# An adaLN block in split fp32: weight work of one pair of f tiles and a row scaling at later points, sums and splits interleaved, and another order of the last token tiles

## The chip, the cores and the metric

The kernel runs on one core of one Trainium2 chip. Its time is the device time of one execution, in microseconds (us). Five engines matter here: TensorE (PE, the matmuls; PEld is its weight loading), VectorE (DVE), ScalarE (ACT), GpSimd (POOL) and SyncE (SP), whose queue issues every DMA of this kernel. Each engine takes its instructions in the order in which they were written and waits, on semaphores, for what an instruction needs; whatever stands behind a waiting instruction on its engine waits too.

## The reference, cut to what matters

A token block of 2048 rows by 512 columns goes through a conditioned layer norm, linear attention, a second layer norm and a bilinear feed-forward network. The change touches the network's last part only:

```python
g = jnp.einsum("bsd,df->bsf", x, w_gate)      # 512 -> 1376
u = jnp.einsum("bsd,df->bsf", x, w_up)
h = g * u
return jnp.einsum("bsf,fd->bsd", h, w_down)   # 1376 -> 512
...
x = x + gb * _B_ref(h, B_w_gate, B_w_up, B_w_down)
```

Here `gb` is a row of 512 numbers. The kernel scales the rows of `w_down` by it once, so that the product needs only to be added to `x`.

## The kernel before, in words

**Tiling.** The 2048 tokens are four chunks of four token tiles (128 rows each); the 1376 columns f are ten tiles of 128 and one of 96, tile 10, which the code calls odd. Everything is fp32, and a matmul takes fp32r operands: each operand is split into a rounded part, written by ACT (`AF.Copy`), and the remainder, a subtraction on DVE or POOL. A product of two split operands is three matmuls. A split is thus ACT first, then DVE or POOL, and both parts go to PE.

**The network** handles two chunks at a time with a seven-product scheme for 2x2 blocks (Strassen-Winograd), so that blocks are summed and subtracted before they are split. `block` (L1174) makes one f tile of h for two chunks in seven products over four PSUM banks a, b, c, d, with 42 matmuls of 512 columns. Between products it calls what is planned for the points p1, p5, p6, p2, p7, p3, p4, in that order in time. The sum at L1218 (`p5 = c + p5`) reads bank c after the fifth product, and the seventh product writes c again, so PE has the length of the sixth product for it.

**The last eleven steps** (numbers 8 to 18 of the network; called step 0 to step 10 here) make h for chunks 2 and 3, in the order f = 10, 8, 9, 0 to 7. Step 0 is the odd tile; steps 1 and 2 are the first pair of f tiles, steps 3 and 4 the second, and so on, five pairs. In the first steps the leftover down products of earlier groups run too, with their sums into x (L943) and stores.

**Weight work.** During these steps `Down.planned` (L1450) prepares `w_down`: for each pair the two raw tiles are loaded (`w_load`), scaled by `gb` (`w_scale`, L1366, DVE), combined into t1 to t4 (`w_sum`, L1380, four subtractions of 256 columns on DVE), split (`w_parts`, L1357 on ACT and L1358 on POOL) and stored to DRAM (`w_park`, SP), since SBUF has no room for all; `w_fetch` brings them back. The line `put(b, point, ...)` names step and point. The odd tile's rows are scaled at L1455 on DVE.

**The last stage**, `Down.run` (L1477), makes the seven products of the second matmul for both chunks. PE works in products of two token tiles (`lo`, `hi`); each token tile takes five pairs times three matmuls of 256 columns, and three more where the odd tile belongs to the product. Two token tiles share one PSUM bank. `add` (L1485, DVE) adds a finished tile to x, and stores follow. The sums of h (`h_sum`, L1413, DVE) and their splits (L196 ACT, L197 DVE) are written between the products; `h_next` does sum and split pair by pair for s2 and s4, where s4 needs s2.

**Buffers.** All tiles in SBUF come from one pool of 94 buffers (`tiles`, L64), given out in the order of the program; a buffer's new user waits for the last readers and writers of the old one. The order is written out by hand: no scheduler moves an instruction.

## Time and profile before

| | |
|---|---|
| median of 3 runs | 543.92 us (543.61 to 544.06) |
| the profiled execution | 543.86 us |
| its span, first to last instruction | 542.2 us |
| PE busy | 535.5 us, 99% of the span |
| DVE, ACT, POOL busy | 407.4, 295.9, 160.7 us |
| DMA | 109.21 MB, mean 201 GB/s |

The span starts 0 at the first instruction; a row of the timeline gives start, length, engine, source line, operation and tiles. A row for several matmuls (x16) starts with the first. A matmul's length in such rows includes its way through the array, during which the next one has already started; so the distance between starts tells what a matmul costs, and that is 0.12 us for one of 256 columns and 0.227 us for one of 512 (17 starts from 388.01 to 391.86).

### The profile page before, as it was taken

To read this page: it belongs to the slowest core of one execution; us is meant where nothing else is said; L and a number is where in the kernel's file an instruction comes from. 1 tells how busy PE (TensorE), PEld (TensorE's weight loads), DVE (VectorE), ACT (ScalarE), POOL (GpSimd) and SP (SyncE) were. 2 spreads that over 40 slices of the span, in tenths; PEclk is the share of its full clock that TensorE was granted. 3 is DMA by queue.
4 is the path that set the end of the run, shared out by engine and by line. 5 is a ranking of instruction groups with operands and counts; after the bars stand their busy time and mean duration, and the time that the engine had idled before them with its cause. 6 is when DMAs were issued, how large, how long until landed. Compare 5 with 4: busy or idle time off the path is not lost. (4 is left out here: it accounts for less than half of the span.)

```text
span 542.2 us, 8140 instructions
## 1 busy us (share of the span) xinstructions
PE 535.5 (99%) x2617; PEld 448.3 (83%) x2617; DVE 407.4 (75%) x688; ACT 295.9 (55%) x557; POOL 160.7 (30%) x169
## 2 busy tenths in 40 slices
PE   8999999999999999999999999999999999999997
PEld 7888787888888878878888888887788888899996
DVE  7897779999989888779765677997745554666762
ACT  3696777648587765577674545444524234353320
POOL 2001010010021220085796566749622313210000
PEclk9999999999999999999999999999999999999999
DMA  8902427220165165947879496893189999689122
GB/s 280 383 35 98 136 93 218 89 68 2 44 195 196 37 213 154 294 142 237 285 215 314 186 318 207 254 371 95 43 299 375 380 382 325 224 296 365 52 79 78
DMA packets 86395, 109.21 MB, mean 201 GB/s; under 512 B 10896, under 2 KB 41616, under 8 KB 86352
## 3 DMA queue, kind: packets, MB, share of 16 engines
q1 hardware_dynamic: 86352, 108.70, 59.8%
q8 instruction: 20, 0.33, 0.2%
q14 instruction: 23, 0.19, 0.1%
HBM read 65.93 MB, written 42.73 MB: 200 GB/s over the span
## 5 line engine op out<-in xcount | busy, mean ns | idle before, releaser
L1156 PE MATMUL bank<-h,w 128*128 128x512 f32 (+1 forms) x630 | 145.7, 390 | 0.4 <-DVE u L1218 0.3
L1156 PEld LDWEIGHTS bank<-h,w 128*128 128x128 f32 (+1 forms) x630 | 116.9, 186 | 27.1 <-DVE u L1218 0.7
L1161 ACT ACTIVATE bank<-bank 128x512 f32<-128x512 f32 (+1 forms) x30 | 17.5, 583 | 73.8 <-PE bank L1156 73.6
L197 DVE TENSOR_TENSOR kl<-u,kh 128x512 fp32r<-128x512 f32 (+1 forms) x43 | 30.6, 743 | 27.8 <-ACT kh L196 23.7
L265 POOL TENSOR_TENSOR rstd<-ve,half 128x2 f32<-128x2 f32 (+3 forms) x13 | 11.8, 910 | 109.0 <-DVE ve L264 45.0
L211 PE MATMUL bank<-w,h 128*128 128x512 f32 x104 | 40.9, 393 | 0.1
L209 PE MATMUL bank<-w,h 128*128 128x512 f32 x104 | 40.9, 393 | 0.0
L210 PE MATMUL bank<-w,h 128*128 128x512 f32 x104 | 40.6, 390 | 0.0
L1156 PE MATMUL acc<-h,w 128*128 128x512 f32 x168 | 38.7, 389 | 0.0
L197 POOL TENSOR_TENSOR w<-raw,w 128x512 fp32r<-128x512 f32 (+1 forms) x15 | 21.6, 1446 | 53.4 <-ACT w L196 47.7
L873 PE MATMUL acc<-w,xh 128*128 128x512 f32 x120 | 37.1, 390 | 0.0
L1156 PEld LDWEIGHTS acc<-h,w 128*128 128x128 f32 x168 | 31.5, 188 | 6.5
L1118 POOL TENSOR_TENSOR w<-raw,w 128x256 fp32r<-128x256 f32 (+3 forms) x22 | 24.8, 1127 | 38.3 <-ACT w L1111 34.1
L943 DVE TENSOR_TENSOR x<-acc,x 128x512 f32<-128x512 f32 x40 | 26.1, 685 | 9.9 <-PE acc L1241 8.2
L1436 PE MATMUL acc<-w,kh 128*128 128x256 f32 (+1 forms) x176 | 31.9, 284 | 0.1
L1118 POOL TENSOR_TENSOR w<-t,w 128x512 fp32r<-128x512 f32 (+1 forms) x22 | 29.9, 1357 | 0.0
L196 ACT ACTIVATE kh<-u 128x512 fp32r<-128x512 f32 (+1 forms) x43 | 24.6, 622 | 8.3 <-DVE u L1413 8.3
L1436 PEld LDWEIGHTS acc<-w,kh 128*128 128x128 f32 (+1 forms) x176 | 27.5, 192 | 0.4 <-ACT kh L196 0.3
L873 PEld LDWEIGHTS acc<-w,xh 128*128 128x128 f32 x120 | 22.5, 188 | 4.6
L416 PE MATMUL acc<-kh,xh 128*128 128x512 f32 x64 | 25.3, 395 | 0.0
L1436 PE MATMUL acc<-w,kl 128*128 128x256 f32 x88 | 25.0, 284 | 0.2 <-DVE kl L197 0.2
L1436 PE MATMUL bank<-w,kh 128*128 128x256 f32 (+1 forms) x136 | 24.7, 284 | 0.5 <-DVE x L1485 0.5
(257 smaller groups left out, 1330.0 us busy)
## 6 DMA issues: line engine op xcount, KB each, us to landing
right<-w SPq DMA_DIRECT2D x56, 256.0 KB, 3.4
w<-right SPq DMA_DIRECT2D x56, 256.0 KB, 5.1
raw<-in_w_mod_dram SPq DMA_DIRECT2D x24, 256.0 KB, 3.7
raw<-in_B_w_down_dram SPq DMA_DIRECT2D x20, 256.0 KB, 4.4
down_t<-w SPq DMA_DIRECT2D x20, 256.0 KB, 5.1
w<-down_t SPq DMA_DIRECT2D x20, 256.0 KB, 4.2
x<-in_A_x_dram SPq DMA_DIRECT2D x16, 256.0 KB, 5.4
down_b<-w SPq DMA_DIRECT2D x15, 256.0 KB, 5.2
```

The costliest lines, as they stand in the source:

```text
L196: nc.scalar.activation(h, src, AF.Copy)
L197: (low or nc.vector).tensor_tensor(l, src, f32(h), op=ALU.subtract)
L209: nc.tensor.matmul(ps, ah, bh, start=i == 0, stop=False)
L210: nc.tensor.matmul(ps, ah, bl, start=False, stop=False)
L211: nc.tensor.matmul(ps, al, bh, start=False, stop=i == n - 1)
L416: nc.tensor.matmul(tacc[k], xh[:, a:b], kh, start=first, stop=False)
L873: nc.tensor.matmul(yps[i], x, y, start=False, stop=k == KD - 1 and x is al, skip_group_check=True)
L943: nc.vector.tensor_tensor(xt[:, a:b], dn[j][:, a:b], xt[:, a:b], op=ALU.add)
L1118: sub = lambda out, x, y: (on or nc.gpsimd).tensor_tensor(out, x, f32(y), op=ALU.subtract)
L1156: mm = lambda x, y, **kw: nc.tensor.matmul(ps, x[:, k], y, skip_group_check=True, **kw)
L1161: nc.scalar.activation(out, x, AF.Copy)
L1436: nc.tensor.matmul(ps, x[:, a:b], y, start=start, stop=False, skip_group_check=True)
```

## The change

Four things are written differently; what is computed is the same, and so is the number of instructions on every engine.

1. The odd tile's scaling (L1455) goes from point p6 of step 0 to point p6 of step 1.
2. For the first pair only (`i == 0`), the weight work stands later. The sums go from p7 of step 1 to p6 of step 2; the split of b11 and b21 from p3 of step 1 to p1 of step 2; that of b22 and t1 from p4 of step 1 to p7 of step 2; that of t2, t3, t4 from p6 and p7 to p4 of step 2. The four stores of b11, b21, b22 and t1 go from p1 and p2 of step 2 to its p4. On SP's queue they keep their place: behind the seven loads of the network's weights for step 3, ahead of the two raw tiles of the second pair.
3. `h_next` writes the next pair's sum ahead of the current pair's remainder on DVE, and from s2's last pair goes over to the first sum of s4.
4. The last product takes token tiles 0, 2, 1, 3 instead of 0, 1, 2, 3, and a tile's sum into x is written behind the next tile's product.

```diff
--- before.py
+++ after.py
@@ -1341,6 +1341,8 @@
 
     HALF = D // 2
 
+    FOLLOWS = {"s2": "s4"}
+
     class Down:
 
         def __init__(self, cs, m, odd):
@@ -1419,9 +1421,19 @@
                 self.parts.setdefault(i, {})[name, "split"] = h, l
 
         def h_next(self, name, *pairs):
+
+            self.ahead(name, pairs[0])
             for i in pairs:
+                h, l = B("kh", dt=F32R), B("kl", dt=F32R)
+                x = self.a(i, name)
+                nc.scalar.activation(h, x, AF.Copy)
+                self.ahead(*((name, i + 1) if i + 1 < self.NI else (FOLLOWS.get(name), 0)))
+                nc.vector.tensor_tensor(l, x, f32(h), op=ALU.subtract)
+                self.parts[i][name, "split"] = h, l
+
+        def ahead(self, name, i):
+            if name and name not in self.parts[i]:
                 self.h_sum(name, i)
-                self.h_split(name, i)
 
         def part(self, bs, j):
             return bs[j // 2][:, j % 2 * HALF:(j % 2 + 1) * HALF]
@@ -1452,20 +1464,26 @@
             def put(b, point, *does):
                 plan.setdefault((self.m + b, point), []).extend(does)
 
-            put(0, "p6", lambda: nc.vector.tensor_tensor(self.odd, self.odd, gb[:self.odd.shape[0]], op=ALU.mult))
+            put(1, "p6", lambda: nc.vector.tensor_tensor(self.odd, self.odd, gb[:self.odd.shape[0]], op=ALU.mult))
             put(1, "p4", *(lambda n=n: self.w_split(("odd", n), self.odd[:, n * HALF:(n + 1) * HALF], nc.gpsimd) for n in range(2)))
             for i in range(self.NI):
                 a, b = 1 + 2 * i, 2 + 2 * i
                 put(a - 1, "p4", lambda i=i: self.w_load(i))
                 put(a, "p1", lambda i=i: self.w_scale(i))
-                put(a, "p7", lambda i=i: self.w_sum(i, "t1", "t3", "t2", "t4"))
-                put(a, "p3", lambda i=i: self.w_parts(i, "b11", "b21"))
-                put(a, "p4", lambda i=i: self.w_parts(i, "b22", "t1"))
-                put(b, "p1", lambda i=i: self.w_park(i, "b11", "b21"))
                 put(b, "p5", lambda i=i: self.h_split("a11", i))
-                put(b, "p6", lambda i=i: self.w_parts(i, "t2", "t3"))
-                put(b, "p2", lambda i=i: self.w_park(i, "b22", "t1"))
-                put(b, "p7", lambda i=i: self.w_parts(i, "t4"))
+                if i:
+                    put(a, "p7", lambda i=i: self.w_sum(i, "t1", "t3", "t2", "t4"))
+                    put(a, "p3", lambda i=i: self.w_parts(i, "b11", "b21"))
+                    put(a, "p4", lambda i=i: self.w_parts(i, "b22", "t1"))
+                    put(b, "p1", lambda i=i: self.w_park(i, "b11", "b21"))
+                    put(b, "p6", lambda i=i: self.w_parts(i, "t2", "t3"))
+                    put(b, "p2", lambda i=i: self.w_park(i, "b22", "t1"))
+                    put(b, "p7", lambda i=i: self.w_parts(i, "t4"))
+                else:
+                    put(b, "p1", lambda i=i: self.w_parts(i, "b11", "b21"))
+                    put(b, "p6", lambda i=i: self.w_sum(i, "t1", "t3", "t2", "t4"))
+                    put(b, "p7", lambda i=i: self.w_parts(i, "b22", "t1"))
+                    put(b, "p4", lambda i=i: self.w_parts(i, "t2", "t3", "t4"), lambda i=i: self.w_park(i, "b11", "b21", "b22", "t1"))
                 if i + 1 < self.NI:
                     put(b + 1, "p1", lambda i=i: self.w_park(i, "t2", "t3", "t4"))
                     put(b + 1, "p5", lambda i=i: self.h_sum("s1", i))
@@ -1545,9 +1563,12 @@
             for j in range(NJ):
                 self.mm(O, j, odd, j % 2 == 0)
             add(c1, 1, O, range(NJ), (HALF, D))
-            for js in (lo, (2,), (3,)):
-                self.product(Y, js, "a22", "t4", False, (1, 0))
-                add(c1, 0, Y, js, (0, HALF))
+            before = []
+            for j in (0, 2, 1, 3):
+                self.product(Y, (j,), "a22", "t4", False, (1, 0))
+                add(c1, 0, Y, before, (0, HALF))
+                before = (j,)
+            add(c1, 0, Y, before, (0, HALF))
 
     def fill(n):
         for _ in range(n):
```

Engine order, first place: DVE in steps 0 and 1. In the kernel before, the odd tile's scaling (L1455, tile raw with row) stands behind the last remainder (h) written ahead of it and in front of the sum L1218 of step 0:

```order
L197 TENSOR_TENSOR h_4187<-f_3822,h_4186 128x512
L1455 TENSOR_TENSOR raw_4067<-raw_4067,row_1562 96x512
L1218 TENSOR_TENSOR u_4184<-bank_2867,u_4184 96x512
L1222 TENSOR_TENSOR u_4197<-bank_2868,u_4197 96x512
L1184 TENSOR_TENSOR u_4197<-bank_2865,u_4197 96x512
L1184 TENSOR_TENSOR u_4184<-bank_2867,u_4184 96x512
```

and the first pair's sums (L1380, tiles t) stand in step 1, behind L1218 and ahead of L1222:

```order
L1218 TENSOR_TENSOR u_4309<-bank_2867,u_4309 128x512
L1380 TENSOR_TENSOR t_4348<-raw_4255 128x256
L1380 TENSOR_TENSOR t_4349<-raw_4257,raw_4255 128x256
L1380 TENSOR_TENSOR t_4348<-raw_4257,t_4348 128x256
L1380 TENSOR_TENSOR t_4349<-raw_4257,t_4348 128x256
L1222 TENSOR_TENSOR u_4318<-bank_2868,u_4318 128x512
L1184 TENSOR_TENSOR u_4318<-bank_2865,u_4318 128x512
L1184 TENSOR_TENSOR u_4309<-bank_2867,u_4309 128x512
```

Now step 1 has the odd scaling (L1467) behind the pair's two scalings, and no sums:

```order
L1368 TENSOR_TENSOR raw_4254<-raw_4254,row_1562 128x512
L1368 TENSOR_TENSOR raw_4256<-raw_4256,row_1562 128x512
L1467 TENSOR_TENSOR raw_4067<-raw_4067,row_1562 96x512
L1218 TENSOR_TENSOR u_4308<-bank_2867,u_4308 128x512
L1222 TENSOR_TENSOR u_4317<-bank_2868,u_4317 128x512
L1184 TENSOR_TENSOR u_4317<-bank_2865,u_4317 128x512
L1184 TENSOR_TENSOR u_4308<-bank_2867,u_4308 128x512
```

and the sums (L1382) stand in step 2, behind the remainder of the split of a11 (kl) and ahead of that step's L1218:

```order
L197 TENSOR_TENSOR kl_4432<-u_4317,kh_4431 128x512
L1382 TENSOR_TENSOR t_4444<-raw_4254 128x256
L1382 TENSOR_TENSOR t_4445<-raw_4256,raw_4254 128x256
L1382 TENSOR_TENSOR t_4444<-raw_4256,t_4444 128x256
L1382 TENSOR_TENSOR t_4445<-raw_4256,t_4444 128x256
L1218 TENSOR_TENSOR u_4429<-bank_2867,u_4429 128x512
L1222 TENSOR_TENSOR u_4442<-bank_2868,u_4442 128x512
L1184 TENSOR_TENSOR u_4442<-bank_2865,u_4442 128x512
L1184 TENSOR_TENSOR u_4429<-bank_2867,u_4429 128x512
```

One row moved by a step, and four rows moved by a step and from behind L1218 to ahead of it.

Second place: DVE in the last stage, at the start of `h_next` for s2 (tiles s are the sums, kl the remainders, x rows the adds). Before, sum and remainder of a pair follow each other:

```order
L1413 TENSOR_TENSOR s_4564<-s_4564,u_4318 128x512
L197 TENSOR_TENSOR kl_5436<-s_4564,kh_5435 128x512
L1413 TENSOR_TENSOR s_4750<-s_4750,u_4573 128x512
L197 TENSOR_TENSOR kl_5441<-s_4750,kh_5440 128x512
L1485 TENSOR_TENSOR x_156<-x_156,acc_4525 128x256
L1485 TENSOR_TENSOR x_158<-x_158,acc_4525 128x256
L1413 TENSOR_TENSOR s_4936<-s_4936,u_4759 128x512
L197 TENSOR_TENSOR kl_5478<-s_4936,kh_5477 128x512
L1413 TENSOR_TENSOR s_5122<-s_5122,u_4945 128x512
L197 TENSOR_TENSOR kl_5483<-s_5122,kh_5482 128x512
L1485 TENSOR_TENSOR x_160<-x_160,acc_4526 128x256
L1485 TENSOR_TENSOR x_162<-x_162,acc_4526 128x256
```

Now the sum of the next pair stands ahead of the remainder of the current one:

```order
L1415 TENSOR_TENSOR s_4564<-s_4564,u_4317 128x512
L1415 TENSOR_TENSOR s_4750<-s_4750,u_4573 128x512
L1431 TENSOR_TENSOR kl_5436<-s_4564,kh_5435 128x512
L1415 TENSOR_TENSOR s_4936<-s_4936,u_4759 128x512
L1431 TENSOR_TENSOR kl_5441<-s_4750,kh_5440 128x512
L1503 TENSOR_TENSOR x_156<-x_156,acc_4525 128x256
L1503 TENSOR_TENSOR x_158<-x_158,acc_4525 128x256
L1415 TENSOR_TENSOR s_5122<-s_5122,u_4945 128x512
L1431 TENSOR_TENSOR kl_5478<-s_4936,kh_5477 128x512
L1415 TENSOR_TENSOR s_5279<-s_5279,u_5131 128x512
L1431 TENSOR_TENSOR kl_5483<-s_5122,kh_5482 128x512
L1503 TENSOR_TENSOR x_160<-x_160,acc_4526 128x256
```

Every remainder has moved down by one sum; the adds keep their places among the remainders.

Third place: DVE at the end (x_156, x_158, x_160 and x_162 are token tiles 0 to 3 of chunk 3; bank_2865 holds tiles 0 and 1, bank_2866 tiles 2 and 3). Before:

```order
L1485 TENSOR_TENSOR x_162<-x_162,bank_2868 128x256
L1485 TENSOR_TENSOR x_156<-x_156,bank_2865 128x256
L1485 TENSOR_TENSOR x_158<-x_158,bank_2865 128x256
L1485 TENSOR_TENSOR x_160<-x_160,bank_2866 128x256
L1485 TENSOR_TENSOR x_162<-x_162,bank_2866 128x256
```

Now:

```order
L1503 TENSOR_TENSOR x_162<-x_162,bank_2868 128x256
L1503 TENSOR_TENSOR x_156<-x_156,bank_2865 128x256
L1503 TENSOR_TENSOR x_160<-x_160,bank_2866 128x256
L1503 TENSOR_TENSOR x_158<-x_158,bank_2865 128x256
L1503 TENSOR_TENSOR x_162<-x_162,bank_2866 128x256
```

The middle two adds have changed places, as the products on PE have; each add now stands behind the product of the following tile in the program.

## The prediction

> **What bounds the kernel now.** I read the head of the page first, then who waits for whom on PE, then PE's timeline where it waits.
>
> ```profile
> PE 535.5 (99%) x2617; PEld 448.3 (83%) x2617; DVE 407.4 (75%) x688; ACT 295.9 (55%) x557; POOL 160.7 (30%) x169
> ```
>
> PE is busy for 99% of the span, so nothing but PE's own waits can be won by a new order. The view of waits, cut to PE, names all of them:
>
> ```profile
> PE acc L146 <- DVE w L141: 2.0, 1, 2.0
> PE bank L1436 <- DVE x L1485: 0.5, 1, 0.5
> PE bank L1156 <- DVE u L1218: 0.3, 1, 0.3
> PE acc L1436 <- DVE kl L197: 0.2, 1, 0.2
> PE bank L1156 <- DVE u L1184: 0.2, 1, 0.2
> ```
>
> The first is the start of the program, which the change doesn't touch. The other four each happen once, all for DVE, and add up to 1.2 us of idle PE. That counts only time in which no matmul is in the array; what PE loses in starts is more. In its timeline the four stand here:
>
> ```profile
> 368.79 3.85 PE L1156 MATMUL bank<-h,w 128*96 128x512 f32 x16
> 372.90 1.63 PE L1156 MATMUL bank<-h,w 128*96 128x512 f32 x6 [0.26 <-DVE u L1218]
> 374.36 0.40 PE L1239 MATMUL acc<-w,kh 128*128 128x512 f32 x1
> ...
> 391.86 0.39 PE L1241 MATMUL acc<-w,kl 128*128 128x512 f32 x1
> 392.43 3.91 PE L1156 MATMUL bank<-h,w 128*128 128x512 f32 x16 [0.18 <-DVE u L1184]
> ...
> 512.50 0.28 PE L1436 MATMUL acc<-w,kl 128*128 128x256 f32 x1
> 512.87 0.50 PE L1436 MATMUL acc<-w,kh 128*128 128x256 f32 x2
> 513.60 0.39 PE L1436 MATMUL acc<-w,kl 128*128 128x256 f32 x1 [0.23 <-DVE kl L197]
> 513.82 0.40 PE L1436 MATMUL acc<-w,kh 96*128 96x256 f32 x2
> ...
> 535.66 0.28 PE L1436 MATMUL bank<-w,kl 96*128 96x256 f32 x1
> 536.45 0.50 PE L1436 MATMUL bank<-w,kh 128*128 128x256 f32 x2 [0.51 <-DVE x L1485]
> 536.79 0.28 PE L1436 MATMUL bank<-w,kl 128*128 128x256 f32 x1
> ```
>
> Sixteen matmuls of 512 columns take 3.85 us with the last one's 0.40, so a start comes every 3.45 / 15 = 0.23 us; of 256 columns every 0.40 - 0.28 = 0.12 us. By these:
>
> - Gap 1, step 0: 372.90 - 368.79 - 16 x 0.23 = 0.43, and the six behind it take 1.46 in place of 1.38: 0.08. Together 0.51 us.
> - Gap 2, end of step 1: 392.43 - 391.86 - 0.23 = 0.34 us.
> - Gap 3, product s4: four starts from 512.50 to 513.82 take 1.32 in place of 0.48: 0.84 us.
> - Gap 4, last token tile: three starts from 535.66 to 536.79 take 1.13 in place of 0.36: 0.77 us.
>
> The sum is 2.46 us. It is what the change can win at most, and each of its four parts stands at one gap.
>
> **The change part by part.** DVE's rows in steps 0 to 3:
>
> ```profile
> 371.02 1.22 DVE L1455 TENSOR_TENSOR raw<-raw,row 96x512 f32<-96x512 f32 x1
> 372.17 0.68 DVE L1218 TENSOR_TENSOR u<-bank,u 96x512 f32<-96x512 f32 x1
> ...
> 382.51 1.28 DVE L1366 TENSOR_TENSOR raw<-raw,row 128x512 f32<-128x512 f32 x2
> 385.59 0.69 DVE L1218 TENSOR_TENSOR u<-bank,u 128x512 f32<-128x512 f32 x1 [1.79 <-PE bank L1156]
> 386.20 1.56 DVE L1380 TENSOR_TENSOR t<-raw 128x256 f32<-128x256 f32 x1
> ...
> 389.12 1.84 DVE L1380 TENSOR_TENSOR t<-raw,t 128x256 f32<-128x256 f32 x2
> ...
> 396.68 0.69 DVE L197 TENSOR_TENSOR kl<-u,kh 128x512 fp32r<-128x512 f32 x1 [2.00 <-issue]
> 399.55 0.69 DVE L1218 TENSOR_TENSOR u<-bank,u 128x512 f32<-128x512 f32 x1 [2.18 <-PE bank L1156]
> ...
> 407.19 1.40 DVE L1366 TENSOR_TENSOR raw<-raw,row 128x512 f32<-128x512 f32 x2 [1.51 <-DMA raw<-in_B_w_down_dram]
> ...
> 411.86 0.69 DVE L1218 TENSOR_TENSOR u<-acc,u 128x512 f32<-128x512 f32 x1 [1.94 <-PE acc L1156]
> 412.47 0.48 DVE L1380 TENSOR_TENSOR t<-raw 128x256 f32<-128x256 f32 x1
> ...
> 413.20 1.34 DVE L1380 TENSOR_TENSOR t<-raw,t 128x256 f32<-128x256 f32 x2
> ```
>
> *The odd scaling.* It ran 1.22 us right ahead of the L1218 that PE waited for; without it L1218 can start up to 1.15 us earlier, at 371.0, ends near 371.8, and PE wants it at 372.90 - 0.43 = 372.47. Gap 1 goes: -0.51 us. At its new place DVE is idle for 1.79 us ahead of L1218; the scaling costs 0.64 there (half of 1.28), at most the 1.22 of its old row. Covered: 0. Without that cover it would cost its length less 1.79, so nothing either way.
>
> *The first pair's sums.* They ran from 386.20 to 389.12 + 1.84 = 390.96, 4.76 us, ahead of L1222 and the two L1184, for which PE waited at 392.43. Without them L1222 and L1184 run when PE releases them. Gap 2 goes: -0.34 us. In step 2 the sums now stand between the remainder that ends at 396.68 + 0.69 = 397.37 and L1218, in a hole of 2.18 us. Their price there isn't in the trace; the nearest rows are those of the second pair, which ran from 412.47 to 413.20 + 1.34 = 414.54: 2.07 us. The other end is the first pair's own 4.76. Behind them wait L1218 and, through it, PE's seventh product. L1218 starts when the fifth product has left the array; the sixth takes 6 x 0.23 = 1.38, L1218 itself 0.69, and the last matmul of the fifth stays about 0.40 - 0.23 = 0.17 in the array beyond its share, so L1218 may be 0.5 us late before PE notices (an estimate from these rows). Sums of up to 2.18 + 0.5 = 2.7 us are thus free. Which end applies is told by POOL and ACT:
>
> ```profile
> 387.44 1.47 POOL L1118 TENSOR_TENSOR w<-t,w 128x512 fp32r<-128x512 f32 x1
> ...
> 398.30 2.14 POOL L1358 TENSOR_TENSOR w<-t,w 128x256 fp32r<-128x256 f32 x3 [4.65 <-ACT w L1357]
> ```
>
> ```profile
> 395.47 0.60 ACT L1161 ACTIVATE u<-bank 128x512 f32<-128x512 f32 x1 [0.74 <-PE bank L1156]
> ...
> 397.80 1.03 ACT L1357 ACTIVATE w<-t 128x256 fp32r<-128x256 f32 x3
> ```
>
> Where the sums were slow, POOL worked on remainders of 512 columns. Where they go, POOL was idle for 4.65 us up to 398.30, since ACT has no rounded part for it before 397.80, and now this is the time of b22 and t1 (p7). Two of POOL's remainders, b11 and b21, are new ahead of it: they follow ACT's two new splits at p1, which fill ACT's idle 0.74 ahead of 395.47 (three splits take 1.03, two about 0.7), so POOL ends them near 397. The sums meet POOL only from 398.30 on, as the second pair's do; I take 2.07, and the cost is 0. The trace thus has 1.56 beside POOL's 1.47, and 0.48 for the same operation apart from it. The Trainium skill, "SBUF — State Buffer", section "Who interferes with whom", says why: a VectorE instruction with two SBUF inputs and a GpSimd instruction that reads SBUF use one port, and whichever starts second is blocked until the other has finished. By my row the cost here is 0; by the strict form of that rule it is the 0.6 us of the second rival below.
>
> *Splits and stores.* ACT has b22, t1, t2, t3, t4 (five, 0.31 apart) from 397.80 on, in place of three: 0.7 us more, with no PE work of ACT's behind it in that step. POOL ends five remainders of 2.14 / 3 = 0.71 near 398.3 + 3.6 = 401.9. SP's queue:
>
> ```profile
> 401.26 0.42 SPq L1389 DMA_DIRECT2D down_t<-w  x1
> 401.94 0.95 SPq L113 DMA_DIRECT2D raw<-in_B_w_down_dram  x2
> ```
>
> SP reaches the store of t1 at 401.26; its remainder is the second of the five and done near 398.3 + 1.4 = 399.7. So SP doesn't wait, and the two raw tiles of the second pair behind it leave as before. DVE does wait for those (1.51 us at 407.19), but has 1.94 us to spare ahead of the L1218 at 411.86; PE being 0.85 us earlier by then leaves 1.1. Cost: 0.
>
> *The interleaving.* Of each pair of s2 and s4 in the last stage, this is the course now:
>
> ```profile
> 500.05 0.69 DVE L1413 TENSOR_TENSOR s<-s,u 128x512 f32<-128x512 f32 x1
> 501.43 0.69 DVE L197 TENSOR_TENSOR kl<-s,kh 128x512 fp32r<-128x512 f32 x1 [0.70 <-ACT kh L196]
> ...
> 512.85 0.69 DVE L197 TENSOR_TENSOR kl<-u,kh 128x512 fp32r<-128x512 f32 x1 [0.76 <-ACT kh L196]
> ...
> 535.97 0.42 DVE L1485 TENSOR_TENSOR x<-x,bank 128x256 f32<-128x256 f32 x1 [1.40 <-PE bank L1436]
> ```
>
> DVE sums, idles 0.70 for ACT's rounded part, subtracts. Ten pairs of s2 and s4 give nine idle times that the next sum fills: 9 x 0.70 = 6.3 us by which the last remainder (512.85) moves ahead, to about 506.5. The adds between may hold it, since they wait for PE. The last two ahead of it wait for the second half of the product of a12. PE's row at 512.50 is the last matmul of s4's fourth pair, so s4 began 11 x 0.12 = 1.3 earlier, at 511.2, and the product of s2 before it takes 4 tiles x 15 matmuls x 0.12 = 7.2: the product of a12 ends at 504.0. Two adds, one sum and two remainders after that (2 x 0.42 + 3 x 0.69 = 2.9) make 506.9, much the same. PE wants the last pair at 512.62 (512.50 + 0.12), and by the two gaps gone both sides move alike. Gap 3 goes: -0.84 us. Behind it the splits of s3 and a22 only move ahead.
>
> *The last tiles.* PE waits at 536.45 since tile 3 shares a bank with tile 2, and the add of tile 2 (0.42 from 535.97) comes first. In the new order each tile's bank was last read during the tile ahead, which takes 18 x 0.12 = 2.16 us against an add of 0.42. Gap 4 goes: -0.77 us. The last tile's add and store stay as they were; the store ahead of it leaves 2.16 us sooner, so nothing is added.
>
> Sum: 0 - 0.51 - 0.34 - 0.84 - 0.77 = -2.46 us on the profiled execution's 543.86: 541.40. That execution is 0.06 under the median of the runs, 543.92, so I predict 541.4.
>
> **The rivals.**
>
> *The sums stay slow.* If the four sums cost in step 2 what they cost in step 1, 4.76, they end at 402.1, L1218 is 4.76 - 2.7 = 2.1 us too late for PE, and the time is 543.5: no change. At the longest row, 4 x 1.56 = 6.24, PE loses 3.5 us: 544.9, slower. It turns from gain to loss at 2.7 + 2.46 = 5.2 us for the four. For it speaks the 1.56 us against 0.48 of the same operation; against it that POOL has only rows of 0.71 there, which begin when the sums are half done. 0.12 (0.07 no change, 0.05 slower).
>
> *The last two sums queue behind POOL.* Two sums at 0.48, and two that each stand behind one whole remainder of POOL: 4 x 0.48 + 2 x 0.71 = 3.3 us, 0.6 over what is free: 542.0. For it speaks that the second pair's last two sums take 1.34 where the first takes 0.48, beside POOL; against it that even so they sum to 2.07. 0.14. It is the case that the page of the Trainium skill cited above describes.
>
> *The gaps are worth only PE's idle time.* If the array's own pace and not the starts decide, 1.2 us come back: 542.7. Against it: the starts behind each gap run on at the old distance and catch up nothing. 0.06.
>
> *PE runs into its weights.* PE is 0.85 us earlier in steps 3 to 10, whose weights come by DMA; if these are just in time, the first two gaps return there as waits for a DMA: 542.3. Against it: PE's waits hold no row for a DMA in the whole span. 0.04.
>
> **How the numbers follow.** The forecast holds 0.64. Faster by over 0.2% (1.1 us, about what these runs can tell from no change) are the forecast, the queue behind POOL, the idle-only case and the weights: 0.88; no change 0.07; slower 0.05. The range goes from 540.9 (the four gaps and the runs' spread of 0.45 us) to 542.9, which takes in the three faster rivals; 0.12 and some of the unknown lie outside.
>
> **What would show it.** Right: PE's waits keep only the start's 2.0 us row; no PE row with an idle time near 372, 392, 512 and 535; the sums between a remainder and L1218 with a total near 2.1 us; the last remainder of s4 before 508; the last four adds 2.16 us apart. Wrong: a PE wait for L1218 in step 2 (near 400), a wait of L1366 for its raw tiles that reaches L1218, or a PE row with a DMA as releaser.

## The result, and the profile after

The changed kernel takes 541.25 us (median of 4, 541.09 to 541.50) against 543.83 (543.61 to 544.06) for the kernel before: a ratio of 0.9956, 95% interval 0.9941 to 0.9971. Measured again beside 23 executions of the kernel before, the ratio is 0.9963 (0.9951 to 0.9975; 541.72 against 543.71). So it is faster by 2.0 to 2.6 us; 541.4 had been predicted. The profiled execution took 541.17 us.

The head of the page after, with PE's line:

```profile
span 539.5 us, 8146 instructions
PE 533.7 (99%) x2617; PEld 447.8 (83%) x2617; DVE 402.6 (75%) x688; ACT 295.8 (55%) x557; POOL 159.5 (30%) x169
```

The view of waits of the kernel after, cut to PE, has one row left, that of the start:

```profile
PE acc L146 <- DVE w L141: 2.0, 1, 2.0
```

PE's timeline of the kernel after at the places of gaps 1 and 2 (start, length, engine, line, operation, tiles, count):

```profile
368.77 4.77 PE L1156 MATMUL bank<-h,w 128*96 128x512 f32 x20
373.38 0.40 PE L1239 MATMUL acc<-w,kh 128*128 128x512 f32 x1
...
395.62 5.15 PE L1156 MATMUL bank<-h,w 128*128 128x512 f32 x22
400.61 0.39 PE L1239 MATMUL acc<-w,kh 128*128 128x512 f32 x1
```

Twenty starts from 368.77 to 373.38, 0.23 us apart, with no idle time; and in step 2, where the sums now are, 22 from 395.62 to 400.61 at the same distance. DVE and POOL in that step, after:

```profile
395.16 0.69 DVE L197 TENSOR_TENSOR kl<-u,kh 128x512 fp32r<-128x512 f32 x1 [3.18 <-ACT kh L196]
395.76 0.42 DVE L1382 TENSOR_TENSOR t<-raw 128x256 f32<-128x256 f32 x1
396.10 0.42 DVE L1382 TENSOR_TENSOR t<-raw,raw 128x256 f32<-128x256 f32 x1
396.44 1.42 DVE L1382 TENSOR_TENSOR t<-raw,t 128x256 f32<-128x256 f32 x2
396.83 0.74 POOL L1360 TENSOR_TENSOR w<-raw,w 128x256 fp32r<-128x256 f32 x1 [1.70 <-ACT w L1359]
397.53 3.02 POOL L1360 TENSOR_TENSOR w<-t,w 128x256 fp32r<-128x256 f32 x4
398.09 0.69 DVE L1218 TENSOR_TENSOR u<-bank,u 128x512 f32<-128x512 f32 x1 [0.23 <-PE bank L1156]
```

The four sums take 396.44 + 1.42 - 395.76 = 2.10 us, and DVE idles 0.23 for PE ahead of L1218: the sums are covered. In the last stage of the kernel after, DVE's timeline shows the last remainder of s4 ending at 503.99 + 1.52 = 505.5 and the last adds 2.16 us apart (the first and the last of the four):

```profile
503.39 0.69 DVE L1415 TENSOR_TENSOR u<-u,s 128x512 f32<-128x512 f32 x1
503.99 1.52 DVE L1431 TENSOR_TENSOR kl<-u,kh 128x512 fp32r<-128x512 f32 x2
...
529.36 0.42 DVE L1503 TENSOR_TENSOR x<-x,bank 128x256 f32<-128x256 f32 x1 [1.41 <-PE bank L1448]
...
535.84 0.42 DVE L1503 TENSOR_TENSOR x<-x,bank 128x256 f32<-128x256 f32 x1 [1.73 <-PE bank L1448]
```

**Where the 2.69 us between the two profiled executions went.** Both kernels issue 2617 matmuls, so PE's starts can be set against each other by number, and the difference read ahead of and behind each place:

| place | after against before | step there |
|---|---|---|
| row at 364 us | -0.48 | -0.48 |
| behind gap 1 (step 0) | -1.00 | -0.52 |
| behind gap 2 (end of step 1) | -1.46 | -0.46 |
| behind gap 3 (product s4) | -2.30 | -0.83 |
| behind gap 4 (last token tile) | -3.06 | -0.76 |
| end of the span | -2.70 | +0.36 |

The four gaps give 2.57 us, near the forecast's 2.46. The first and the last row of the table weren't in the forecast. Up to step 0 the two programs are the same, so the 0.48 us of the first row cannot come from the change. The experiments go after both, and after what makes the gaps.

### The profile page after: what moved, and what is told of

It reads as the page before. It is cut to its first block, busy times and chain, and to the rows that moved or that the text cites. A ratio compares the mean times of both kernels' runs of the same rounds, so it can differ in the third digit from the quotient of the medians.

```text
span 539.5 us, 8146 instructions
## 1 busy us (share of the span) xinstructions
PE 533.7 (99%) x2617; PEld 447.8 (83%) x2617; DVE 402.6 (75%) x688; ACT 295.8 (55%) x557; POOL 159.5 (30%) x169
## 4 chain that ended last, share of the span: by engine, by line
PE 94%; DVE 3%; SPq 1%; issue 1%; DMA 0%; ACT 0%; DVEq 0%
PE bank L1156 27%; PE acc L873 8%; PE acc L1156 7%; PE acc L1448 6%; PE bank L1448 5%; PE bank L211 4%; PE bank L209 3%; PE bank L210 3%; PE acc L1239 3%; PE acc L1240 3%; PE acc L1241 3%; PE acc L416 2%; PE acc L418 2%; PE bank L956 2%; PE bank L958 2%; PE acc L417 2%
## 5 line engine op out<-in xcount | busy, mean ns | idle before, releaser
L197 DVE TENSOR_TENSOR kl<-u,kh 128x512 fp32r<-128x512 f32 (+1 forms) x38 | 26.5, 735 | 25.4 <-ACT kh L196 23.3
L418 PE MATMUL acc<-kl,xh 128*128 128x512 f32 x64 | 25.0, 391 | 0.0
L417 PE MATMUL acc<-kh,xl 128*128 128x512 f32 x64 | 25.0, 390 | 0.0
L1239 PE MATMUL acc<-w,kh 128*128 128x512 f32 x64 | 24.9, 389 | 0.0
```

Of the source, the lines that this page charges most:

```text
L197: (low or nc.vector).tensor_tensor(l, src, f32(h), op=ALU.subtract)
L417: nc.tensor.matmul(tacc[k], xl[:, a:b], kh, start=False, stop=False)
L418: nc.tensor.matmul(tacc[k], xh[:, a:b], kl, start=False, stop=last)
L1239: nc.tensor.matmul(ps, hh[:, a:b], dh[:n, c:d], start=i == 0, stop=False)
```

## The experiments

The theory is that of the forecast: the time follows PE's starts, and the change removes four waits of fixed size. The rivals: only PE's idle time counts; the sums stay slow in step 2 since POOL blocks them; a gap moves elsewhere. Each ratio is to the kernel before, run beside the experiment: its median was 543.25 us beside the four single parts, 543.71 or 543.41 beside the others. PE's rows are set against those of the kernel before by number, as in the table.

### The odd scaling alone

```diff
-            put(0, "p6", lambda: nc.vector.tensor_tensor(self.odd, self.odd, gb[...], op=ALU.mult))
+            put(1, "p6", lambda: nc.vector.tensor_tensor(self.odd, self.odd, gb[...], op=ALU.mult))
```

> The kernel before with only the odd tile's scaling moved from step 0 to step 1. By the forecast gap 1 (step 0, near 372.9) goes and nothing else: PE's rows behind it stand 0.51 us earlier against the rows ahead of it, the median is 543.3, and the scaling takes 0.64 to 0.7 in step 1 without a new wait of PE. If only PE's idle time is won: 0.26 us, 543.6. If the scaling at its new place holds PE up there: a new PE wait in step 1, 543.8 or more. The gaps near 392, 512.5 and 536.4 stay in each case.

Measured: 542.94 us against 543.25, ratio 0.9996 (0.9987 to 1.0004), which cannot be told from no change; the rows tell more. Gap 1 is gone, as forecast. But gap 2 is gone as well, though the sums still stand in step 1, and gap 3 has grown from 0.84 to 1.18 us. Neither was expected by any theory; both are taken up below. The scaling takes 0.68 us in step 1.

### The first pair's weight work alone

```diff
-                put(a, "p7", lambda i=i: self.w_sum(i, "t1", "t3", "t2", "t4"))
...
+                else:
+                    put(b, "p1", lambda i=i: self.w_parts(i, "b11", "b21"))
+                    put(b, "p6", lambda i=i: self.w_sum(i, "t1", "t3", "t2", "t4"))
...
```

> The kernel before with only the first pair's sums, splits and stores moved into step 2. By the forecast gap 2 (end of step 1, near 392.4) goes: 0.34 us by the forecast's own working, 0.46 by how far PE's rows moved there in the changed kernel; median 543.4; the four sums take about 2.1 us in step 2 and PE does not wait there; VectorE's adds of x at the end of step 1 come about 3 us sooner, so the sync engine's queue leaves sooner and VectorE's wait of 1.51 us for the raw tiles near 407 shrinks or goes. If only idle time is won: 0.18, 543.6. If the sums are short in step 2 only because the odd scaling has left step 0: a PE wait for L1218 near 400 and 543.8 or more.

Measured: 542.89 against 543.25, 0.9989 (0.9980 to 0.9997). Gap 2 is gone and the others stay (gap 1 with 0.56 us of lost starts). The sums take 2.10 us in step 2, and DVE's wait for the raw tiles is gone: the adds of x come at 389.05 in place of 392.80, the stores behind them leave sooner, and with them the sync engine's queue. DVE's timeline of this kernel, where the kernel before waited 1.51 us:

```profile
404.61 1.29 DVE L1366 TENSOR_TENSOR raw<-raw,row 128x512 f32<-128x512 f32 x2
...
410.88 0.69 DVE L1218 TENSOR_TENSOR u<-acc,u 128x512 f32<-128x512 f32 x1 [3.65 <-PE acc L1156]
```

With the other parts alone that wait stays (1.35 us with the scaling moved, 1.59 with the interleaving).

### The interleaving alone

```diff
+                self.ahead(*((name, i + 1) if i + 1 < self.NI else (FOLLOWS.get(name), 0)))
+                nc.vector.tensor_tensor(l, x, f32(h), op=ALU.subtract)
...
-                self.h_split(name, i)
```

> The kernel before with only the sums of s2 and s4 interleaved with their remainders. By the forecast gap 3 (512.5 to 513.8) goes: 0.84 us, median 543.0; the last remainder of s4 moves from 512.85 to about 506.5. If only idle time is won: 0.23, 543.6. If the adds that wait for PE hold the remainders instead, the last one stays near 512 and the gap with it: 543.8.

Measured: 542.65 against 543.25, 0.9987 (0.9978 to 0.9995); PE's rows behind gap 3 move by 0.84. But this kernel's steps 0 and 1 have the instructions of the kernel before, and its profile has gap 1 and not gap 2.

### The order of the last tiles alone

```diff
-            for js in (lo, (2,), (3,)):
-                self.product(Y, js, "a22", "t4", False, (1, 0))
-                add(c1, 0, Y, js, (0, HALF))
+            before = []
+            for j in (0, 2, 1, 3):
+                self.product(Y, (j,), "a22", "t4", False, (1, 0))
+                add(c1, 0, Y, before, (0, HALF))
+                before = (j,)
+            add(c1, 0, Y, before, (0, HALF))
```

> The kernel before with only the last four token tiles in the order 0, 2, 1, 3, the add of each behind the product of the next. By the forecast gap 4 (536.45) goes: 0.77 us, median 543.1; the last adds stand 2.16 us apart. If only idle time is won: 0.51, 543.3. If what follows the last add is bound by the stores ahead of it and not by the last add, PE ends 0.77 sooner but the span does not: 543.8.

Measured: 542.47 against 543.25, 0.9983 (0.9974 to 0.9992). Gap 4 is gone: PE's rows move by 0.76. This kernel too has steps 0 and 1 as before, and here gap 2 is there and gap 1 is not.

The four medians give 0.31 + 0.36 + 0.60 + 0.78 = 2.05 us, less than the 2.57 of the table. The times alone don't show that anything is missing: by their ratios the four give 0.0045, or 2.4 us, and each ratio is uncertain by 0.0009, or 0.5 us. What shows it are the rows of the last two kernels.

**Gaps 1 and 2 are not there in every execution.** DVE and POOL in step 1 of the kernel with the interleaving alone:

```profile
385.73 1.59 POOL L1118 TENSOR_TENSOR w<-raw,w 128x512 fp32r<-128x512 f32 x1
385.74 0.41 DVE L1382 TENSOR_TENSOR t<-raw 128x256 f32<-128x256 f32 x1
386.08 1.52 DVE L1382 TENSOR_TENSOR t<-raw,raw 128x256 f32<-128x256 f32 x1
387.28 1.47 POOL L1118 TENSOR_TENSOR w<-t,w 128x512 fp32r<-128x512 f32 x1
387.52 2.38 DVE L1382 TENSOR_TENSOR t<-raw,t 128x256 f32<-128x256 f32 x2
```

and POOL's row of the kernel before, beside which its first sum started at 386.20 and took 1.56:

```profile
386.19 1.28 POOL L1118 TENSOR_TENSOR w<-raw,w 128x512 fp32r<-128x512 f32 x1
```

Both times POOL's row starts some 10 ns ahead of the sum, too close for the starts to tell which goes first; the lengths tell it. In one execution the sum goes first and POOL takes 1.59 in place of 1.28; in the other POOL goes first and the sum takes 1.56 in place of 0.41. The four sums come to 4.16 us in the one (387.52 + 2.38 - 385.74) and 4.76 in the other, and that 0.60 decides gap 2. It is also why gap 2 was gone with the scaling alone, where the sum started 0.03 ahead:

```profile
385.25 0.41 DVE L1380 TENSOR_TENSOR t<-raw 128x256 f32<-128x256 f32 x1
385.28 1.54 POOL L1118 TENSOR_TENSOR w<-raw,w 128x512 fp32r<-128x512 f32 x1
```

The same kernel with one fill more (below) has a first sum of 0.42 and no gap 2 either. Whether the scaling ahead of it in step 1 favours that order, two profiles can't show. Gap 1 is decided in the same way, three instructions ahead of the scaling. DVE, POOL and PE in step 0 of the kernel with the last tiles alone, where gap 1 is absent:

```profile
366.78 1.29 DVE L197 TENSOR_TENSOR kl<-u,kh 128x512 fp32r<-128x512 f32 x2 [1.70 <-ACT kh L196]
367.45 1.22 POOL L1100 TENSOR_TENSOR t<-raw 128x256 f32<-128x256 f32 x1 [6.51 <-DMA raw<-in_B_w_up_dram]
...
370.29 1.22 DVE L1455 TENSOR_TENSOR raw<-raw,row 96x512 f32<-96x512 f32 x1
...
370.68 3.17 PE L1156 MATMUL bank<-h,w 128*96 128x512 f32 x13
...
371.44 0.68 DVE L1218 TENSOR_TENSOR u<-bank,u 96x512 f32<-96x512 f32 x1
```

and the two rows at the same place of the kernel before:

```profile
366.96 1.84 DVE L197 TENSOR_TENSOR kl<-u,kh 128x512 fp32r<-128x512 f32 x2 [1.49 <-ACT kh L196]
367.11 1.14 POOL L1100 TENSOR_TENSOR t<-raw 128x256 f32<-128x256 f32 x1 [5.78 <-PE bank L1156]
```

Two remainders take 1.29 us where POOL starts after the second of them, and 1.84 where it starts 0.46 ahead of it. The 0.55 is as much as all of gap 1: L1218 starts 0.73 earlier here, 0.18 of which PE has from the start as well, and 13 matmuls of PE run on without a wait, with the scaling still in its old place and still 1.22 long. Of the profiles whose step 0 is that of the kernel before, three have gap 1 and one has not; of those whose steps 0 and 1 both are, two have gap 2 and one has not.

### POOL's reading taken away

```diff
+    class Fill:
+        def tensor_tensor(out, x, y, op):
+            for _ in range(2):
+                nc.gpsimd.memset(f32(out), 0.0)
...
-            rights[n].sums(on)
+            rights[n].sums(Fill if n >= FIRST_AGAIN - 2 else on)
...
-            rights[n].lows(on)
+            rights[n].lows(Fill if n >= FIRST_AGAIN - 2 else on)
```

> The kernel before, with POOL's sums and remainders of the gate and up weights for the two steps behind step 0 replaced by two fills with zero each, which read nothing; these weights are then wrong and the output with them. The odd scaling and the first pair's sums stay where they were. If POOL's reading is what doubles VectorE's rows there, L1455 takes 0.68 in place of 1.22, the first two sums 0.42 each, gaps 1 and 2 are both gone, and the time is 0.3 to 1.0 us under the kernel before. If the scaling and the sums are simply too much work ahead of L1218 and L1184, the gaps stay: no change.

Measured: 543.09 against 543.71, 0.9991 (0.9982 to 1.0000): 0.62 us, with 0.36 more lost in gap 3 by the pause of DVE that is told of below. Its DVE and POOL rows in step 0, and PE's:

```profile
369.04 0.68 DVE L1462 TENSOR_TENSOR raw<-raw,row 96x512 f32<-96x512 f32 x1
369.24 3.83 POOL L1277 MEMSET w<- 128x256 f32 x8
...
370.75 2.69 PE L1156 MATMUL bank<-h,w 128*96 128x512 f32 x11
```

The scaling (here L1462) takes 0.68 beside a busy POOL that reads nothing, and both gaps are gone with the scaling and the sums in their old places. So POOL's reading made the rows long, not POOL being busy and not the amount of work (this kernel leaves out POOL's sums and remainders of two steps' weights and has zeros in their place). Of the first two sums I had expected 0.42 each; they took 0.93 and 0.96, since POOL, done sooner, was by then at its remainders L1365 of the odd tile and the first pair, which do read.

### The sums written twice

```diff
-                    put(b, "p6", lambda i=i: self.w_sum(i, "t1", "t3", "t2", "t4"))
+                    put(b, "p6", *[lambda i=i: self.w_sum(i, "t1", "t3", "t2", "t4")] * 2)
```

> The changed kernel with the first pair's four sums written twice in step 2 (the same values again). The forecast says that sums of up to 2.7 us are free there. Eight sums come to about 0.42 x 6 + 1.4 = 3.9 us, or more where VectorE stands behind POOL: L1218 is then about 1.6 late against the 0.23 that VectorE had idle, and PE, which the forecast lets notice after another 0.5, loses about 1.0 us near 399 and runs 0.1 slow behind it: 1.0 us above the changed kernel. If the hole is wider than the forecast says: no PE wait, no change. If PE notices at once: 1.5.

Measured: 542.57 against the changed kernel's 541.72 beside it. From its timeline:

```profile
396.15 0.42 DVE L1382 TENSOR_TENSOR t<-raw 128x256 f32<-128x256 f32 x1
...
398.82 1.35 DVE L1382 TENSOR_TENSOR t<-raw,t 128x256 f32<-128x256 f32 x2
...
400.09 0.68 DVE L1218 TENSOR_TENSOR u<-bank,u 128x512 f32<-128x512 f32 x1
...
400.83 1.67 PE L1156 MATMUL bank<-h,w 128*128 128x512 f32 x6 [1.04 <-DVE u L1218]
```

Eight sums take 398.82 + 1.35 - 396.15 = 4.02 us, and PE's starts show a wait of 1.20 us ahead of that row and 0.12 behind it. So 4.02 - 1.20 = 2.8 us are free there; the forecast had 2.7. The time rose by 0.85 and not 1.32: 0.36 at the program's end went (below), and the 0.1 left is within the scatter.

### POOL kept busy beside the sums

```diff
+        def pool_work(self, i, times):
+            for _ in range(times):
+                nc.gpsimd.tensor_tensor(wide[:, 0], *self.raw[i], op=ALU.subtract)
...
-                    put(b, "p1", lambda i=i: self.w_parts(i, "b11", "b21"))
+                    put(b, "p1", lambda i=i: self.w_parts(i, "b11", "b21"), lambda i=i: self.pool_work(i, 3))
```

> The changed kernel with three more instructions of POOL in step 2, ahead of the four sums, each with two inputs of 512 columns out of SBUF (their result is not used). If POOL's instructions are what makes VectorE's sums slow, the four sums take 4.2 to 4.8 us again, as in step 1 of the kernel before, PE waits for L1218 by 1.6 to 2.2 us near 400, and the time is that much above the changed kernel. If the sums are slow or fast for another reason (their place, the kind of tile): 2.1 us, no PE wait, no change of the time.

Measured: 545.61 us (544.30 to 546.66), ratio to the kernel before 1.0033 (1.0021 to 1.0046): the gain is lost and more. From its timeline:

```profile
395.52 4.43 POOL L1372 TENSOR_TENSOR wide<-raw,raw 128x512 f32<-128x512 f32 x3
395.60 1.77 DVE L197 TENSOR_TENSOR kl<-u,kh 128x512 fp32r<-128x512 f32 x1 [3.18 <-ACT kh L196]
397.29 1.51 DVE L1386 TENSOR_TENSOR t<-raw 128x256 f32<-128x256 f32 x1
...
400.16 1.80 DVE L1386 TENSOR_TENSOR t<-raw,t 128x256 f32<-128x256 f32 x2
...
402.62 1.65 PE L1156 MATMUL bank<-h,w 128*128 128x512 f32 x6 [2.77 <-DVE u L1218]
```

The sums take 400.16 + 1.80 - 397.29 = 4.67 us, within the expected 4.2 to 4.8. PE loses 3.05 us of starts (2.93 of them in the wait), more than the 1.6 to 2.2 expected, because I had left out the remainder ahead of the sums: it took 1.77 in place of 0.69. With that 1.08 the two together are 5.75, and 5.75 - 2.93 = 2.8 us were free once more. The other executions of this kernel are up to 2.4 us slower than the profiled one (544.30). Their granted clock is lower, 0.994 to 0.997 against 0.999, and falls as their time rises; 0.005 of 544 is 2.7 us, an estimate that covers it. So the price of the blocked sums is the 3.05 of the trace and not the difference of the medians. What lowered the clock stays open.

### Order and bank of the last tiles apart

```diff
-            for j in (0, 2, 1, 3):
+            for j in range(NJ):
```

> The changed kernel with the last token tiles in the order 0, 1, 2, 3 again, each add still behind the product of the next tile. If it is the add's place and not the bank that makes PE wait, there is no gap near 536; but the add of tile 2 now waits for the product of tile 3, which shares its bank, so two adds and two stores stand behind PE's last matmul in place of one: 0.33 for the other add and about 0.4 for the issue of the other store, so the span ends 0.3 to 0.4 us later behind PE's last matmul than in the changed kernel. If the shared bank itself is what costs: PE's gap of 0.77 us stays.

Measured: 541.93 us (541.45 to 542.35), 0.9973 (0.9963 to 0.9984). There is no gap. Its last two adds stand together behind PE's last matmul:

```profile
535.58 0.75 DVE L1503 TENSOR_TENSOR x<-x,bank 128x256 f32<-128x256 f32 x2 [3.56 <-PE bank L1448]
```

From PE's last start to the end of the span it takes 4.48 us against 3.94 in the changed kernel: 0.54 more, where 0.3 to 0.4 was expected. So gap 4 goes with the later add alone, and the alternation saves the 0.54 behind it that the later add would cost.

### One interleaved pair

```diff
-            self.h_next("s4", 3, 4)
+            self.h_last("s4", 3, 4)
...
+        def h_last(self, name, i, j):
+            self.h_sum(name, i)
...
+            self.h_sum(name, j)
+            nc.vector.tensor_tensor(l, self.a(i, name), f32(h), op=ALU.subtract)
...
```

> The changed kernel with the interleaving for the last pair of s4 alone; the other nine pairs go sum, rounding, remainder as before. The forecast had nine idle times of 0.70 us filled and the last remainder at 506.5. By the rows of before, swapping this one sum takes its 0.69 and its idle 0.70 out of the last chain: the last remainder comes 1.39 us earlier, which is more than the 0.84 of gap 3: gap 3 is gone with one of nine, and the time is that of the changed kernel. If the whole lead is needed: a PE wait near 510 of 0.1 to 0.8 us stays.

Measured: 541.26 us (540.92 to 541.91), 0.9963 (0.9950 to 0.9976): no PE wait behind the first 11 us, with nine of ten pairs as they were before. DVE's rows:

```profile
507.83 1.29 DVE L1413 TENSOR_TENSOR u<-u,s 128x512 f32<-128x512 f32 x2
509.29 0.69 DVE L1431 TENSOR_TENSOR kl<-u,kh 128x512 fp32r<-128x512 f32 x1 [0.18 <-ACT kh L1429]
509.90 0.69 DVE L197 TENSOR_TENSOR kl<-u,kh 128x512 fp32r<-128x512 f32 x1
```

The last remainder starts at 509.90. PE is 1.52 earlier here than in the kernel before, whose last remainder would stand at 512.85 - 1.52 = 511.33, so it came forward by 1.43 us (1.39 expected).

### A pause of 0.36 us, and where it lies

Two differences were left: the changed kernel's end, 3.94 us behind PE's last start in place of 3.58, and the larger gap 3 with the scaling alone.

```diff
     nc.gpsimd.memset(half, -0.5)
+    nc.gpsimd.memset(half, -0.5)
...
-    keep_on(24)
+    keep_on(19)
```

> The changed kernel with one more fill of 4 columns on POOL at the start and 19 in place of 24 idle matmuls of PE ahead of its first real one. In both profiles of the changed kernel POOL stands still for 0.36 us between two of the program's last semaphores (PE's last start to the end is 3.94 us against 3.57 to 3.59 in all other kernels), and its stream has 330 instructions there, one fewer than any kernel without that pause. If the pause hangs on where in POOL's stream the instruction lies, one instruction more moves it: 3.58. If it belongs to the changed last stage: 3.94. The fewer idle matmuls let the first real one start up to 1.1 us sooner, of which the work behind it may give back all; PE's row at 15 us tells: 0 to 0.5 us. The time is 0.36 to 0.8 under the changed kernel, or the same.

Measured: 541.20 us (541.04 to 541.70), 0.9961 (0.9948 to 0.9973). The end is 3.58. The lines view shows it on the last four semaphore instructions of POOL, in the second profile of the changed kernel:

```profile
L1833 POOLq EVENT_SEMAPHORE  x4: 17/17/17, 539.0 to 539.9; - x4
```

and in this kernel:

```profile
L1834 POOLq EVENT_SEMAPHORE  x4: 17/17/17, 538.7 to 539.2; - x4
```

They are 0.9 us apart in the first and 0.5 in the second, with nothing between that POOL waits for; 0.29 of it lies between the first two. With one more fill of 4 columns at the program's start, half a millisecond earlier, it is gone. (That the number of instructions is the same on every engine, as said of the change, holds for the working ones. With those that only handle semaphores POOL has 332 records before the change and 330 after it.) Every profile with 330 records on POOL has the pause (the changed kernel twice, and the two kernels before this one), and none of those with 331 to 339, all but this one with the 24 idle matmuls. Beside the changed kernel's two medians, 541.25 and 541.72, a gain of this size can't be told apart; the trace alone shows it. The first real matmul starts at 8.69 us, but PE's row near 23 us stands at 22.89 against 22.74 and 22.95 in the two profiles of the changed kernel. The five idle matmuls less gave nothing.

```diff
     nc.vector.tensor_copy(idle, idle_f)
+    spare = consts.tile([P, NJ], F32, name="spare")
+    nc.vector.memset(spare, 0.0)
...
-            put(0, "p6", lambda: nc.vector.tensor_tensor(self.odd, ...))
+            put(1, "p6", lambda: nc.vector.tensor_tensor(self.odd, ...))
```

> The kernel before with the odd scaling in step 1, as in the first experiment, and one more small fill on VectorE at the start. There gap 3 grew from 0.84 to 1.18 us: VectorE stood still for 0.35 more ahead of a remainder of s2 at 493, with nothing that it waited for. Its stream had 901 instructions, as in the other kernel with this pause, against 902 in the kernel before. If the pause hangs on where in the stream the instruction lies: it is gone, gap 3 is 0.84 again, and the idle time ahead of that remainder 0.75. If it comes from PE being 1 us earlier: 1.1 and 1.18 again.

Measured: 542.78 against 543.41, 0.9988 (0.9979 to 0.9997). DVE's timeline at the remainder of s2, in the kernel with the scaling alone:

```profile
493.08 0.69 DVE L197 TENSOR_TENSOR kl<-s,kh 128x512 fp32r<-128x512 f32 x1 [1.10 <-issue]
```

and with the fill as well:

```profile
492.81 0.69 DVE L199 TENSOR_TENSOR kl<-s,kh 128x512 fp32r<-128x512 f32 x1 [0.75 <-issue]
```

The pause is gone, and gap 3 is 0.84 again. Of the seven profiles that keep this order of sums and remainders, the two with the pause (the scaling alone, and POOL's fills) have 831 of DVE's records ahead of that remainder, and the five without it 832 or 833. So the pause hangs on where in an engine's stream an instruction stands. What the engine does in it, no run here shows.

### The changed kernel once more

> The changed kernel as it is, once more, beside many runs of the kernel before. The four single parts gave 0.31, 0.36, 0.60 and 0.78 us by their medians, 2.05 together, since gaps 1 and 2 are not there in every execution: one of two executions of the same instructions had gap 1 and not gap 2, another gap 2 and not gap 1. By that theory the change is worth about 2.0 us here (ratio 0.9963), and its profile has no wait of PE behind the start in any execution. If all four gaps were always there: 2.57 us (0.9953).

Measured: 541.72 us (541.66 to 541.84), ratio 0.9963 (0.9951 to 0.9975): the first of the two numbers expected. Its profile has no wait of PE behind the start. With gap 1 in three of four profiles, gap 2 in two of three, gaps 3 and 4 always and the pause paid, the change is worth 0.52 x 3/4 + 0.45 x 2/3 + 0.84 + 0.77 - 0.36 = 1.9 us, a rough estimate from so few profiles; measured 2.0. With all four gaps always there and the pause paid it would be 2.57 - 0.36 = 2.2, which the interval (1.4 to 2.7 us) doesn't rule out: that two gaps come and go is shown by the rows, not by this time. The first comparison gave 2.58, 0.4 more than both gaps and the pause explain. Its four executions of each kernel are few, and the start alone differs by more than that from one execution to the next (below); more I can't show.

## Why the prediction was right, and where it was not

The time (541.4 against 541.25 and 541.72) and the sign were right, and the range held. By its steps:

- **Gap 3, 0.84:** right (0.83 and 0.84). The last remainder starts at 504.8 and ends at 505.5 with PE 1.46 us earlier, so at 506.3 and 507.0 in the time of the kernel before (506.5 for its start and 506.9 for its end were forecast). That nine idle times were needed was never said, but the sum was made of them; one is enough.
- **Gap 4, 0.77:** right (0.76 twice). "Nothing is added" behind it held for the store.
- **Gap 1, 0.51:** the size was right (0.52 and 0.56), the reason half right. L1218 was late because the scaling and the rows ahead of it were doubled by POOL; without the scaling L1218 ended at 371.5 (371.8 predicted, with PE 0.48 later), but in an execution where POOL started a little later it was in time with the scaling. The step that failed is "it ran 1.22 us right ahead of the L1218 that PE waited for", taken as the scaling's own length: its own is 0.68.
- **Gap 2, 0.34:** mis-sized; 0.46 by the shift of PE's rows. The working for gap 1 had counted the slow starts behind a wait, that for gap 2 had not (0.09). And it too is absent in some executions.
- **The sums in step 2, 2.07 and free up to 2.7:** 2.10, and 2.8 by two experiments. One reading was off: the sum of 1.56 stood beside POOL's row of 1.28 at 386.19, and not beside its 1.47 at 387.44.
- **Splits and stores:** "DVE does wait for those" failed: the load of the raw tiles left 3 us sooner and DVE had 3.65 us to spare, not 1.1. I had followed the sync engine's queue from the moved stores on, and not from the store of x ahead of them, which waits for adds that the sums had held up. "SP doesn't wait" failed as well: the stores waited for POOL for 1.4 us in that stretch, at no cost.
- **The rivals:** "the last two sums queue behind POOL" had the right mechanism. In the changed kernel one of four sums stands behind POOL (0.97 us for it by the trace), too little to pass 2.8. "The sums stay slow" gave its price as 2.1 to 3.5 us; with POOL kept busy PE lost 3.05. That only PE's idle time counts fell with gaps 3 and 4, whose 0.84 and 0.77 came back whole. No weight's transfer held PE up.

The number came out so close partly by luck. On the two profiled executions the sum of the four, 2.57, stands beside 0.48 that came ahead of step 0 and 0.36 lost at the end. Over many executions the four are worth about 2.3 and not 2.46, by the rough estimate above. The forecast took the gaps of one profile as fixed parts of the program; two of the four were the outcome of a start some 10 ns or 0.5 us sooner or later.

## What to carry to other kernels

A wait seen in one profile can be an accident of that execution: before costing it, see whether the rows ahead of it have a length that the same operation doesn't have elsewhere, and what POOL reads beside them. Price a moved DVE instruction with two SBUF inputs by its length apart from POOL, and then ask which POOL instructions can start just ahead of it at its new place. When PE has no slack, look for the one pair of instructions that ends the chain; here swapping that pair did away with the gap as swapping all ten did.

## What the runs showed of the hardware that was not expected

**One goes first, and the other waits it out.** A DVE instruction with two SBUF inputs and a POOL instruction that reads SBUF don't slow each other in shares: one takes its own time and the other is longer by most of that (POOL by 0.3 us beside the sum's 0.41, the sum by 1.15 beside POOL's 1.28). The sum of 256 columns took 0.41 or 1.56 beside the same POOL row, which took 1.59 or 1.28. A POOL that only fills did nothing to DVE (0.68), and DVE's L1218, which has one of its inputs in PSUM, took 0.68 beside POOL's 1.18 in the kernel before. The Trainium skill, "SBUF — State Buffer", section "Who interferes with whom", has this as an exclusive lock; the lengths in these runs agree. What the forecast's reading of it lacked is that which of the two goes first, and so the price, changes from one execution to the next.

**An engine can pause for 0.36 us at a place of its stream.** It is seen at one place on DVE (1.10 in place of 0.75 idle) and at one on POOL (0.36 at the end). One instruction more ahead of the place did away with it both times. An edit that changes an engine's count by one can so move the time by a third of a microsecond at a place it doesn't touch.

**The start differs from execution to execution.** The timeline's row of the 24 idle matmuls at the start, in the kernel before:

```profile
2.00 8.48 PE L146 MATMUL acc<-w 128*128 128x512 f32 x24 [2.00 <-DVE w L141]
```

and in the changed one:

```profile
2.00 7.72 PE L146 MATMUL acc<-w 128*128 128x512 f32 x24 [2.00 <-DVE w L141]
```

Their starts are 0.43 us apart at first and 0.23 later, and the change comes between 5.0 and 8.0 us in the profiles here. At 364 us PE's row stands at 363.68 to 364.50 in kernels that are alike up to there but for the start's five idle matmuls and fills. Not all of these 0.8 us come from the start: the kernel with the scaling alone was 0.74 ahead of the kernel before at 23 us and 0.40 at 364, and what gave back the rest stays open. That the rate switches at a time of its own, by a window that doesn't begin with the kernel, is what the Trainium skill says ("TensorE: Matmul & The Clock Gate", section "Part 1: The HAM clock gate"). The runs show that the time varies; the window itself they don't show. The difference is about the size of one of the parts that were predicted, so single profiles were compared by the shift at each place and not by their spans.
